# Squared-ReLU attention and gated block: seven-product sums for 6 instead of 4 of 12 column blocks, in-place squares, half-batch values, one list of units

## The chip, the cores and the metric

The kernel runs on one core of a Trainium2 chip. The metric is device time in microseconds for one execution. Before the change the median of three runs is 408.92 us (408.41 to 411.5).

## The reference

```python
# attention: batch 8, heads 12, sequence 448, head size 64
scores = matmul(q, k.transpose(0, 1, 3, 2)) / sqrt(64)
attn = maximum(scores, 0) ** 2 / 448
x = matmul(attn, v)          # laid out as (3584 tokens, 768)
# gated block: w_gate, w_val (768, 1536), w_out (1536, 768)
g = x @ w_gate
gelu = 0.5 * g * (1 + erf(g / sqrt(2)))
out = (gelu * (x @ w_val)) @ w_out
```

All inputs and the output are float32; the kernel loads them as bf16 and accumulates in float32.

## The kernel before

Work goes by batch of 448 tokens. Every matmul uses one 64x64 quarter of the TensorE array (`mm`, L299): two row halves, called PE0 and PE1 in the code, and two column halves, so that four matmuls can run side by side.

For each batch there are 21 score units (`add_scores`, L597). Each fills one PSUM tile `sp` with the scores of 896 columns; ACT takes the ReLU of it (L634, tile `rl`), DVE squares two units at once (a *duo*, L646, tile `attnT`). Six value units (`add_values`, L678) multiply the squares by v; each gives 128 of the 768 rows of x transposed, copied and scaled into `xT` (L709 on DVE or L720 on ACT). q and k of a third of a batch (4 heads) are transposed on TensorE for batches 0 and 1 (L567), and from batch 2 on by a regrouping copy on DVE (L402, `qkr`) and a transposing DMA on SP's queue (L407, `qkT`).

The gate and value products have 12 column blocks of 128 per batch. A dense block of one batch is two units (`add_gate_value`, L901) of 24 matmuls of 448 columns each: the gate unit ends in a gelu on ACT (L922), the value unit in a multiplication on DVE (L927), which writes the block into `uT`. From batch 2 on (`ALONE = 2`) two neighbouring batches form a pair, and for the first 4 blocks (`2 * NP`, `NP = 2`) both batches together are computed as a 2x2 block product in seven units (`add_pair`, L795) of 12 matmuls. These use sums of weights (`add_pair_sums`, L755, `ws`) and sums of x (`add_token_sums`, L773, `ts`). Units 1, 6, 5 and 3 accumulate one after another in one PSUM bank (stage X), 7 and 4 in a second (Y), 2 in a third (Z). After each unit the bank is read: 1, 6 and 7 are copied to `part` on ACT (L843), 2, 4 and 5 are added to `part` on DVE (L847), gelus are taken on ACT (L851) and multiplied on DVE (L856). The first unit of a stage waits for all six values of the second batch (L835).

The output product goes over 14 groups of 256 tokens (`add_product`, L1042), each in seven units of 24 matmuls of 384 columns, with weight sums (`add_weight_sums`, L948, L961), sums of `uT` (`add_sums`, L986, L1026), copies to `osb` on ACT (L1110), additions on DVE (L1108) and stores on SP's queue (L1125). `uT` has room for two batches, so writing batch b waits until the products of batch b - 2 have read theirs.

The order is made before anything runs. `run_plan` (L74) simulates the engines with the costs and lags written in the code and emits instructions in the order of its simulated time. TensorE's units come from a list `later`, sorted by a due time `at`: from the first 40 (`AHEAD`) it takes the first that is ready, or else the one that is ready soonest (`next_unit`, L108). The text `LINE` (L12) gives the order of the gate, value, pair and product units; a digit is the next dense unit of that batch, `2A1` is unit 1 of block A of the pair starting at batch 2, and `a7` is unit 7 of output group a. Score and value units get their due times from a formula and the numbers in `SHIFT` (L1209 to L1239). There are 6 PSUM banks for products and one score tile, once the second score tile has been given up early in the run.

Loads are issued on POOL's queue in the order of L1141 to L1171: batches 0 and 1 mixed with the gate and value weights, then the output weights, then batches 2 to 7 by thirds, each held back until its buffer is free and until a given ReLU has run.

```python
load_w12(4)
load_w12(5)
for i in range(FC // WOG):
    load_wo(i)
add_weight_sums()

late = [(b, m) for b in range(2, B) for m in range(NM)]
```

Of the kernel before, what the change touches and what calls it, by code (L numbers as in the profile page):

```python
# [12 lines left out]
0 0 0 0 0 0 0 0 0 0 0 0 0 a7 0 0 0 0 0 1 1 0 0 1 0 1 0 1 0 1 0 1 1 1 a1 1 1 b1 1 2 a6 a4 a5 1 1 c1 1  # L13
1 1 1 2 1 1 1 a2 2 1 a3 1 1 c6 b6 c7 b7 b5 b2 2 2 c4 2 2 c5 2 2 b3 b4 2 2 3 c2 2A1 2A6 2A7 3 2B1 3
c3 2A2 2B7 2 3 3 2A5 2 2B2 2 2B6 3 2B5 2D1 2D2 2B4 3 2 2C1 2C2 2 3 3 2A3 2C7 2D7 2C6 2B3 2D6 2D5 3
2A4 2D3 2C4 2D4 3 d1 3 3 d6 d7 3 e7 d2 d5 e1 e2 3 e6 e4 d4 2C5 d3 e5 4 4 2C3 3 4 f1 e3 f2 f7 f6 f4
g1 g7 4 f5 g6 g5 4 4 g3 4 g2 4 f3 4B1 5 4 4 5 5 4B2 5 5 4A1 4A2 4B7 g4 4 4B6 4A7 5 4 4 4 4B5 5 4 4
4D1 4A6 5 4C1 4C2 4C6 4D2 4D7 5 5 4C7 4D6 4C5 4D5 5 4C4 4B4 4D4 4A5 5 4A4 i1 4B3 h7 5 h1 5 4D3 h6
4A3 5 4C3 5 h2 i2 h5 i6 h3 i7 6B1 6 j1 6 6B2 6A1 h4 6 6A7 7 i5 6B7 j2 6 6D1 6 6B6 6 6 i3 6A2 7 6 7
i4 7 6 6 6A6 6B5 6 7 6D6 6 7 6 6C7 j7 6 6D2 6D7 j6 6D5 7 6C1 7 j5 6B3 6D3 6A5 6C6 6C2 6C5 6 j4 6D4  # L20
k1 6C4 6 6B4 7 j3 6C3 6A4 k7 l7 l1 7 7 k6 6A3 7 k2 l6 l5 l3 k5 k3 l4 k4 l2 7 7 7 m1 7 n1 m7 m6 n7 m5
n6 m4 m2 n4 n5 m3 n3 n2
# [3 lines left out]
SHIFT = "8 1 7 -2 1.5 1 2.5 -15 5 -3.5 -2.5 -5.5"  # L26


class Op:


    def __init__(self, engine, cost, emit, deps=(), lag=0.0, prio=0, other=None):
        self.engine, self.cost, self.emit, self.prio = engine, cost, emit, prio
        self.deps = [d for d in deps if d is not None]
        self.lag = lag
        self.other = other
        self.takes = None
        self.margin = 0.0
        self.after = None
        self.start = self.end = self.known = self.blocked = None  # L40


class Ring:


    def __init__(self, size, lag=0.0):
        self.size, self.lag, self.ends, self.keys = size, lag, [], set()

# [6 lines left out]
    def take(self, last, key=None):  # L55
        if key is None or key not in self.keys:
            self.ends.append(last)
            self.keys.add(key)


class Unit:


    def __init__(self, at, los, his, box=None, closer=None, prev=None):
        self.at, self.los, self.his, self.box, self.closer, self.prev = at, los, his, box, closer, prev
        self.begun = False
        self.short = False


AHEAD = 40  # L70
BANK = 0.3


def run_plan(queues, pools, units, banks, arrivals, together, fill):  # L74

# [5 lines left out]
    units.sort(key=lambda u: u.at)  # L81
    fixed = len(queues["PE0"])

    def ready(op):
        if op.known is not None:
            return op.known
        if op.blocked is not None and op.blocked.end is None:
            return None
        t = 0.0
        if op.after is not None:  # L90
            if op.after.start is None:
                return None
            t = op.after.start
        if op.takes is not None:
            x = op.takes[0].free(*op.takes[2:])
            if x is None:
                return None
            t = max(t, x)
        for d in op.deps:
            if d.end is None:  # L100
                op.blocked = d
                return None
            t = max(t, d.end + d.lag + (op.margin if d.engine == "SP" else 0.0))
        if op.takes is None:
            op.known = t
        return t

    def next_unit(short):  # L108
        best = None
        now = max(free["PE0"], floor)  # L110
        for u in units[:AHEAD]:
# [3 lines left out]
            if t is None:  # L115
                continue
# [29 lines left out]
    left = sum(map(len, queues.values())) + sum(len(u.los) + len(u.his) for u in units)  # L146
    left += len({id(op) for ops in pools.values() for op in ops})
    while left:
# [16 lines left out]
        for e, ops in pools.items():  # L165
            mine = None
            for op in ops[:48]:
                r = ready(op)
                if r is not None:
                    t = max(r, free[e], floor if e in together else 0.0)  # L170
                    key = (t, op.prio, free[e])
                    if mine is None or key < mine[0]:
                        mine = (key, e, op)
            if mine and (best is None or mine[0] < best[0]):
                best = mine
        assert best is not None, "the plan is stuck"
        (t, _, _), e, op = best
        if isinstance(op, tuple):
            _, u, k = op
            u.begun = True  # L180
            units.remove(u)
            if k is not None:
# [3 lines left out]
            pools["PE1"] += u.his  # L186
# [16 lines left out]
        else:  # L203
            pools[e].remove(op)
            if op.other is not None:
                for x in ("ACT", "DVE"):
                    if x != e:
                        pools[x].remove(op)
        if op.takes is not None:
            op.takes[0].take(*op.takes[1:])  # L210
        op.emit()
        last = max(last, op.end)
# [5 lines left out]
def kernel(  # L218
# [10 lines left out]
    nc = tc.nc  # L229
# [10 lines left out]
    NM = NPAIR // 2  # L240
    NU = SC * NPAIR // 2
# [24 lines left out]
    xpool = ctx.enter_context(tc.tile_pool(name="xpool", bufs=2))  # L266
    upool = ctx.enter_context(tc.tile_pool(name="upool", bufs=2))
    tpool = ctx.enter_context(tc.tile_pool(name="tpool", bufs=RING_T))
    lpool = ctx.enter_context(tc.tile_pool(name="lpool", bufs=2))
    hpool = ctx.enter_context(tc.tile_pool(name="hpool", bufs=RING_H))  # L270
    spool = ctx.enter_context(tc.tile_pool(name="spool", bufs=2))
    rpool = ctx.enter_context(tc.tile_pool(name="rpool", bufs=RING_R))
# [3 lines left out]
    npool = ctx.enter_context(tc.tile_pool(name="npool", bufs=1))  # L276
# [8 lines left out]
    warm = npool.tile([128, 3 * 512], bf16, name="held", tag="held")[:, 0:512]  # L285
# [107 lines left out]
    def add_dma_transposes(b, m, deps=()):  # L393
# [21 lines left out]
        copy = Op("DVE", 0.62, emit_copy, [wait, *(regrouped[n - 2] if n > 1 else ())], lag=0.15, prio=1)  # L415
# [41 lines left out]
    def next_scores(at):  # L457

        n = len(units)
        if at > WIDE and n % SB == 0 or wide:  # L460
            if not wide:
                wide.append(0)
                until.update({FB: at, FB + 1: at})
# [28 lines left out]
    def both(at, ops, scores=False):  # L492

        ops = list(ops)
        if at > FIXED:
# [3 lines left out]
            later.append(Unit(at, [lo for lo, _ in ops], [hi for _, hi in ops], prev=last_scores[0]))  # L499
# [7 lines left out]
    def then(at, step, los, his, box=None, closer=None):  # L507

        if not isinstance(at, list) and at > FIXED:
# [3 lines left out]
            later.append(Unit(at, los, his, box, closer))  # L513
# [35 lines left out]
    def add_transposes(at, b, m, rs):  # L549
# [23 lines left out]
        n, last = next_scores(at) if b else (0, [])  # L573
# [19 lines left out]
        both(at, both_ops)  # L593
# [3 lines left out]
    def add_scores(at, b, u):  # L597
# [7 lines left out]
        n, free = next_scores(at)  # L605
# [25 lines left out]
        def emit_relu():  # L631
            if first:
                duo["rl"] = rpool.tile([128, 2, 2, S], bf16, name="rl", tag="rl")
            relu.ins = nc.scalar.activation(  # L634
                duo["rl"][:, u % 2, :, :], box[0][:, :, 0:S], AF.Relu).ins

        def emit_sq():
            if alone and not first:
                a = duo["a"]
            else:  # L640
                a = duo["a"] = apool.tile([128, 2, 2, S], bf16, name="attnT", tag="attnT")
# [4 lines left out]
            nc.vector.tensor_tensor(a[:, part], duo["rl"][:, part], duo["rl"][:, part], op=ALU.mult)  # L646
# [26 lines left out]
        both(at, zip(*ops))  # L673
# [4 lines left out]
    def add_values(at, b, pr):  # L678
# [24 lines left out]
        def x_tile():  # L703
            if b not in xT:
                xT[b] = xpool.tile([128, KC, S], bf16, name="xT", tag="xT")
            return xT[b][:, pr, :]
# [29 lines left out]
        else:  # L736
            then(at, 0.0, *ops, box, lambda: x_op[b, pr])
# [10 lines left out]
    PLACE5 = -7.0  # L748

    ws, ws_op, ts, ts_op, ts_used = {}, {}, {}, {}, {}  # L750
    K3 = KC // 2
    KTOP, KEND = slice(0, K3), slice(K3, KC)
    ALONE = 2

    def add_pair_sums(i):  # L755

        for n in (1, 2, 4):
# [602 lines left out]
```

## Time and profile before

| What | Value |
|---|---|
| Median of three runs | 408.92 us |
| Span of the profiled execution, first to last instruction | 406.2 us |
| Mean granted TensorE clock | 0.997 |
| TensorE busy | 396.6 us, 8554 matmuls |
| TensorE weight loads | 349.0 us |
| VectorE (DVE) busy | 282.1 us, 480 instructions |
| ScalarE (ACT) busy | 240.7 us, 359 instructions |
| GpSimd (POOL) busy | 73.7 us |
| DMA | 44.86 MB, 110 GB/s on average |

The page gives no time of its own for the profiled execution beside its span; the median of the timed runs is 2.7 us longer than that span. Busy times are shares of the same 406.2 us, and the engines work side by side. A TensorE record lasts from a matmul's start to its modelled end, and several overlap, so "busy" says only that at least one was under way. In the lists, a line number is that of the code, a name such as `ff<-xT,wg` is the written tile and the read ones, and the brackets behind an instruction give the idle time ahead of it on its engine and what ended it.

### The profile page before, as it was taken

How to read it: one execution, taken by the hardware profiler on the slowest of the kernel's cores; microseconds unless marked ns; L12 is line 12 of the kernel's file. 1: busy time of each engine (PE TensorE's matmuls, PEld its weight loads, DVE VectorE, ACT ScalarE, POOL GpSimd, SP SyncE). 2: the span in 40 equal slices, each digit the busy share in tenths (PEclk: the TensorE clock that was granted, in tenths of full speed). 3: DMA queues.
4: the chain of work that ended last, by engine and by line, in shares of the span. 5: the costliest groups of instructions: out<-in, count | busy, mean ns of one | idle time of the engine just before them, and what ended most of it. 6: DMA issues, size and time to landing. Idle time of an engine off the chain costs nothing.

```text
span 406.2 us, 18670 instructions
## 1 busy us (share of the span) xinstructions
PE 396.6 (98%) x8554; PEld 349.0 (86%) x8554; DVE 282.1 (69%) x480; ACT 240.7 (59%) x359; POOL 73.7 (18%) x120
## 2 busy tenths in 40 slices
PE   7899999999999999999999999999999999999995
PEld 3457788889998888999999999998999889889994
DVE  3884787549896688869677787658786765566352
ACT  5856872276676778885556678666546744443130
POOL 7655520211212122121111212020110000000000
PEclk9999999999999999999999999999999999999998
DMA  7999999979899999964779699471323302100416
GB/s 103 184 199 198 197 210 163 120 107 133 108 149 178 165 154 106 110 88 58 96 139 144 113 184 146 69 115 33 48 30 81 79 4 55 29 2 4 135 27 157
DMA packets 75279, 44.86 MB, mean 110 GB/s; under 512 B 36160, under 2 KB 71744, under 8 KB 75200
## 3 DMA queue, kind: packets, MB, share of 16 engines
q0 software_dynamic: 37152, 24.39, 44.9%
q1 hardware_dynamic: 37888, 19.08, 27.2%
q8 instruction: 67, 1.10, 1.1%
q10 hardware_dynamic: 160, 0.20, 0.2%
q14 instruction: 12, 0.10, 0.1%
HBM read 48.76 MB, written 11.01 MB: 147 GB/s over the span
## 4 chain that ended last, share of the span: by engine, by line
PE 93%; DMA 4%; POOL 1%; ACT 0%; issue 0%; SPq 0%; POOLq 0%
PE ff L300 83%; PE sp L300 8%; DMA qkT<-qkr 2%; DMA qk<-in_k_dram 2%; PE ff L488 1%; PE sp L567 1%; POOL qk L355 1%; PE ff L567 1%; ACT rl L634 0%; ACT gel L922 0%; ACT osb L1110 0%; POOL ident masks.py:199 0%; POOL ident masks.py:197 0%; SPq L407 0%; POOLq L1344 0%
## 5 line engine op out<-in xcount | busy, mean ns | idle before, releaser
L300 PE MATMUL ff<-xT,wg 64*64 64x448 bf16 x2016 | 210.1, 349 | 0.0
L300 PE MATMUL ff<-xT,wv 64*64 64x448 bf16 x1728 | 191.1, 349 | 0.0
L634 ACT ACTIVATE rl<-sp 128x896 bf16<-128x896 f32 x168 | 151.9, 921 | 53.5 <-PE sp L300 47.8
L300 PEld LDWEIGHTS <-wv 64*64 64x64 bf16 x2016 | 122.0, 107 | 10.5
L300 PEld LDWEIGHTS <-wg 64*64 64x64 bf16 x2016 | 121.6, 106 | 10.6
L646 DVE TENSOR_TENSOR attnT<-rl 128x1792 bf16<-128x1792 bf16 (+1 forms) x98 | 91.8, 953 | 17.8 <-ACT rl L634 16.2
L300 PE MATMUL ff<-attnT,v 64*64 64x448 bf16 (+1 forms) x768 | 85.8, 326 | 0.3
L300 PEld LDWEIGHTS <-s 64*64 64x64 bf16 x1344 | 77.8, 107 | 2.5 <-issue 0.3
L300 PE MATMUL sp<-qkT 64*64 64x448 bf16 (+1 forms) x768 | 73.4, 328 | 1.5 <-DMA qkT<-qkr 0.8
L922 ACT ACTIVATE gel<-ff 128x448 bf16<-128x448 f32 x72 | 39.1, 543 | 48.0 <-PE ff L300 47.8
L927 DVE TENSOR_TENSOR uT<-gel,ff 128x448 bf16<-128x448 bf16 x72 | 44.4, 619 | 31.6 <-PE ff L300 24.5
L300 PE MATMUL ff<-wo,s 64*64 64x384 bf16 x672 | 61.3, 323 | 0.0
L300 PE MATMUL ff<-wt,s 64*64 64x384 bf16 x672 | 54.9, 323 | 0.0
L300 PE MATMUL ff<-wo,uT 64*64 64x384 bf16 x576 | 54.8, 322 | 0.0
L300 PEld LDWEIGHTS <-uT 64*64 64x64 bf16 x912 | 53.5, 107 | 1.4
L370 POOL DMA_DIRECT2D v<-in_v_dram x48 | 29.5, 619 | 128.2 <-ACT rl L634 49.1
L300 PEld LDWEIGHTS <-v 64*64 64x64 bf16 x768 | 46.5, 107 | 6.2 <-issue 2.5
L1110 ACT COPY osb<-ff 128x384 f32<-128x384 f32 x56 | 26.8, 479 | 37.9 <-PE ff L300 35.8
L300 PEld LDWEIGHTS <-qkT 64*64 64x64 bf16 x768 | 36.2, 106 | 9.0 <-issue 4.8
L709 DVE TENSOR_SCALAR xT<-ff 128x448 bf16<-128x448 f32 x48 | 29.7, 622 | 13.4 <-PE ff L300 12.7
L1108 DVE TENSOR_TENSOR osb<-ff,osb 128x384 f32<-128x384 f32 x42 | 23.4, 556 | 18.4 <-PE ff L300 15.0
L300 PE MATMUL ff<-ts,ws 64*64 64x448 bf16 x288 | 33.4, 349 | 0.0
(57 smaller groups left out, 340.0 us busy)
## 6 DMA issues: line engine op xcount, KB each, us to landing
out_dram<-osb SPq DMA_DIRECT2D x54, 192.0 KB, 3.6
v<-in_v_dram POOLq DMA_DIRECT2D x48, 128.0 KB, 5.1
qk<-in_q_dram POOLq DMA_DIRECT2D x23, 224.0 KB, 5.3
qk<-in_k_dram POOLq DMA_DIRECT2D x23, 224.0 KB, 6.4
wg<-in_moe_w_gate_dram POOLq DMA_DIRECT2D x6, 384.0 KB, 10.2
wv<-in_moe_w_val_dram POOLq DMA_DIRECT2D x6, 384.0 KB, 11.2
wo<-in_moe_w_out_dram POOLq DMA_DIRECT2D x4, 576.0 KB, 14.9
qkT<-qkr SPq DMA_TRANSPOSE x36, 5.2
```

The source lines that it names most:

```text
L300: return nc.tensor.matmul(o, lhsT, rhs, start=start, stop=stop, skip_group_check=onto, tile_position=(P * row, P * col))
L355: op = load(4 * (h1 - h0) * S * D, lambda: nc.gpsimd.dma_start(tile_of(), src[b, h0:h1].rearrange("h (p c) d -> p h (c d)", c=SC)), deps, ...
L370: return nc.gpsimd.dma_start(v16[b, m][HALF[i], :, :, :], v[b, h0:h1].rearrange("h (p c) d -> p h c d", c=SC)[:, :, c0:c0 + VC, :])
L488: nc.tensor.matmul(t[:, :], warm[:, 0:128], warm[:, :], start=True, stop=True)
L567: nc.tensor.transpose(t[HALF[j], c, :], src[:, 2 * r + j, c, :], ident[:, :], tile_position=(0, P * j))
L634: relu.ins = nc.scalar.activation(duo["rl"][:, u % 2, :, :], box[0][:, :, 0:S], AF.Relu).ins
L646: nc.vector.tensor_tensor(a[:, part], duo["rl"][:, part], duo["rl"][:, part], op=ALU.mult)
L709: nc.vector.tensor_scalar_mul(x_tile(), box[0][:, 0:S], scalar1=out_scale)
L922: nc.scalar.activation(gel[b, fc][:, :], box[0][:, 0:S], AF.Gelu)
L927: u_op[b, fc].ins = nc.vector.tensor_tensor(uT[b][:, fc, :], gel.pop((b, fc))[:, :], box[0][:, 0:S], op=ALU.mult).ins
L1108: ins = nc.vector.tensor_tensor(o, box[0][:, 0:OGS], o, op=ALU.add)
L1110: ins = nc.scalar.copy(o, box[0][:, 0:OGS])
```

## The change

- `NP` goes from 2 to 3: blocks 0 to 5 of each pair are computed in seven units, and blocks 6 to 11 densely.
- ReLU writes into the `attnT` tile, and DVE squares it there. The `rl` tiles are gone; a ReLU waits for the values that read its buffer last. Batch 0 has a ring of 5 such buffers in a pool that is later given to the new weight sums and to the token sums; after that the ring is 4.
- `xT` is kept in half batches in a ring of 5 instead of whole batches in a ring of 2.
- The output weights are loaded ahead of the third (2, 2) on POOL's queue, behind the q and k of thirds (2, 0) and (2, 1) and v of (2, 0).
- The copies to `part` and to `osb` may go to ACT or to DVE, by the planner's choice.
- `LINE` now holds every unit behind the start, `s` being the next score unit and `o` the next value unit; the due times and `SHIFT` are gone. The planner takes units from the first 60 of the list and skips those whose buffers could not come free in the order chosen so far.

```diff
-0 0 0 0 0 0 0 0 0 0 0 0 0 a7 0 0 0 0 0 1 1 0 0 1 0 1 0 1 0 1 0 1 1 1 a1 1 1 b1 1 2 a6 a4 a5 1 1 c1 1
...
+0 1 4A1 s 1 s 1 0 o 2 5 1 1 o d1 s 4C5 1 1 1 0 o 0 0 c5 s 2C1 s s o 3 s 0 s a1 s 0 1 2B4 o 5 2 g2
+o s 3 0 2 b7 s 1 o 6B6 o s s s a5 a7 s 4B1 2 d4 s 0 0 0 0 o s 0 a2 4D1 2C7 s s s o 2E1 2A5 0 2C6 s
...
-SHIFT = "8 1 7 -2 1.5 1 2.5 -15 5 -3.5 -2.5 -5.5"
-AHEAD = 40
+AHEAD = 60
 BANK = 0.3
+SPARE = 1
...
             t = ready(u.los[0])
             if t is None:
                 continue
+            if any(op.takes[0].stuck(op.takes[2] if len(op.takes) > 2 else None, sure, n)
+                   for n, op in enumerate(u.grabs)):
+                continue
+            if any(not x.begun for op in u.wants for x in units_under(op) if x is not u):
+                continue
+            if u.chain is not None and u.box is not None and len(opened) >= len(banks) - SPARE:
+                continue
...
+    WO_AT = 2, 2, 2, 2
 
-    NP = 2
-    RING_V, RING_T, RING_H, RING_R, RING_A, RING_O = 3, 3, 2, 2, 4, 4
-    RING_M, RING_G = 5, 4
+    NP = 3
+    RING_V, RING_T, RING_H, RING_L, RING_A, RING_O, RING_E = 3, 3, 2, 2, 4, 4, 5
+    RING_M, RING_G, RING_X = 5, 4, 5
...
         def emit_relu():
             if first:
-                duo["rl"] = rpool.tile([128, 2, 2, S], bf16, name="rl", tag="rl")
+                duo["a"] = (apool if b else sb["first"]).tile([128, 2, 2, S], bf16, name="attnT", tag="attnT")
             relu.ins = nc.scalar.activation(
-                duo["rl"][:, u % 2, :, :], box[0][:, :, 0:S], AF.Relu).ins
+                duo["a"][:, u % 2, :, :], box[0][:, :, 0:S], AF.Relu).ins
...
-            nc.vector.tensor_tensor(a[:, part], duo["rl"][:, part], duo["rl"][:, part], op=ALU.mult)
+            nc.vector.tensor_tensor(a[:, part], a[:, part], a[:, part], op=ALU.mult)
...
-        old = duos[n_d - RING_R] if n_d >= RING_R else None
-        relu = Op("ACT", 0.845, emit_relu, [ops[0][-1], ops[1][-1], *(old["sq"] if old else ())],
-                  lag=0.18, prio=2)
+        relu = Op("ACT", 0.845, emit_relu, [ops[0][-1], ops[1][-1]], lag=0.18, prio=2)
...
-            if b not in xT:
-                xT[b] = xpool.tile([128, KC, S], bf16, name="xT", tag="xT")
-            return xT[b][:, pr, :]
+            h, dc = divmod(pr, K3)
+            if (b, h) not in xT:
+                xT[b, h] = xpool.tile([128, K3, S], bf16, name="xT", tag="xT")
+            return xT[b, h][:, dc, :]
...
         if name in "167":
-            rd = Op("ACT", 0.5, emit_copy, [last], lag=0.2, prio=0)
+            rd = Op("ACT", 0.5, emit_copy, [last], lag=0.2, prio=0,
+                    other=("DVE", 0.58, lambda: emit_copy(nc.vector.tensor_copy)))
...
         rd = Op(engine, 0.52 if added else 0.45, emit_read,
-                [ops[1][-1], *([st["read", before]] if before else ())], lag=0.2, prio=0)
+                [ops[1][-1], *([st["read", before]] if before else ())], lag=0.2, prio=0,
+                other=None if added else ("DVE", 0.52, lambda: emit_read(nc.vector.tensor_copy)))
...
-    for i in range(FC // WOG):
-        load_wo(i)
-    add_weight_sums()
-
     late = [(b, m) for b in range(2, B) for m in range(NM)]
     for n, (b, m) in enumerate(late):
+        for i in range(FC // WOG):
+            if WO_AT[i] == n:
+                load_wo(i)
         for i in range(2):
             load_qk(b, i, 4 * m, 4 * m + 4)
         for b_, m_ in late[n - 1:n] + (late[n:] if n == len(late) - 1 else []):
             load_v(b_, 4 * m_, 4 * m_ + 4)
+    add_weight_sums()
...
-    for new, old in zip(duos[RING_A:], duos):
+    n = (NU + 1) // 2
+    for new, old in [*zip(duos[RING_E:n], duos), *zip(duos[n + RING_A:], duos[n:])]:
         gone = [o_op[b, pr] for keys in old["of"] for b, pr, _ in keys]
-        for sq in new["sq"]:
-            sq.deps += gone
+        for relu in new["relu"]:
+            relu.deps += gone
...
-        op.deps += reads_x.get(b - 2, ())
+        op.deps += reads_x.get(old_half(b, pr), ())
...
+    for u in later:
+        if u.name[0] == "o":
+            b = u.name[1]
+            u.los[0].gates += reads_x.get(old_half(b, u.name[2]), ())
+        elif u.name[0] == "p" and u.name[2] in "17":
+            u.los[0].gates += [u_op[b, f] for tile in sums[u.name[1]]["chunks"] for b, _ in tile for f in range(FC)]
```

More of the change, by code (lines that the diff above doesn't have):

```diff
@@ L39, in __init__ @@
         self.after = None
[L40 removed]
+        self.gates = []
+        self.start = self.end = None
+        self.place = 0
+        self.open = False
 class Ring:
@@ L181, in run_plan @@
             units.remove(u)
+            for x in u.grabs:
+                x.takes[0].ask(*x.takes[1:])
+            if u.chain is not None:
+                opened.add(u.chain)
+                if u.name[-1] in "234":
+                    opened.discard(u.chain)
             if k is not None:
@@ L203, in run_plan @@
         else:
[L204 to L208, printed above, removed]
+            for x in homes[op]:
+                able[x].remove(op)
         if op.takes is not None:
@@ L1178 @@
+    for at, _, fn, args in work:
+        fn(at, *args)
+    names = {}
+    for u in later:
+        names.setdefault(u.name[:2] if u.name[0] == "o" else u.name, []).append(u)
+    flow = {str(b): [("g", *x) for x in dense[b]] for b in range(B)}
+    flow["0"] = flow["0"][2:]
+    flow["s"] = [("s", b) for b in range(B) for _ in names.get(("s", b), ())]
+    flow["o"] = [("o", b) for b in range(B) for _ in names.get(("o", b), ())]
     line = []
```

375 lines of the change are left out of this document (223 added, 152 removed).

## The prediction

> **What bounds the kernel now.** I read the page's first and fourth parts, the timeline of an undisturbed stretch, the groups by shape, and the busy time by windows, in that order. The page says that TensorE is busy almost throughout and that the chain that ended last runs over it for 93% of the span:
>
> ```profile
> span 406.2 us, 18670 instructions
> ...
> PE 396.6 (98%) x8554; PEld 349.0 (86%) x8554; DVE 282.1 (69%) x480; ACT 240.7 (59%) x359; POOL 73.7 (18%) x120
> ...
> PE 93%; DMA 4%; POOL 1%; ACT 0%; issue 0%; SPq 0%; POOLq 0%
> ```
>
> A busy PE is not a full PE here, because a matmul uses one 64x64 quarter of the array and four can run together. The timeline gives the price when all four do (start, duration, instruction):
>
> ```profile
> 67.57 0.38 PE L300 MATMUL ff<-xT,wg 64*64 64x448 bf16 x2
> ...
> 67.61 0.35 PE L300 MATMUL ff<-xT,wv 64*64 64x448 bf16 x2
> ...
> 67.76 0.38 PE L300 MATMUL ff<-xT,wg 64*64 64x448 bf16 x2
> ...
> 67.80 0.35 PE L300 MATMUL ff<-xT,wv 64*64 64x448 bf16 x2
> ```
>
> Each half of the array starts a new pair every 0.19 us, so a 64x448 matmul costs 0.19 / 4 = 47 ns of the array although its record is 349 ns long. By columns, a 384-column one costs 40.5 ns. The counts by shape (5616 of 448 columns, 384 of 224, 2352 of 384) then make 265 + 9 + 95 = 369 us, and the transposes some 6 us more: 375 us of real work up to the last matmul at 401. So about 26 us are lost. The windows (length, PE busy and records, PEld, DVE, ACT, POOL, clock) show where:
>
> ```profile
> 20.00:30.00 10.00, 9.85 (x152) 5.47 (x149) 8.22 (x16) 5.73 (x8) 5.79 (x9) 1.00 1.38 199
> 30.00:40.00 10.00, 10.00 (x210) 7.49 (x207) 4.77 (x8) 5.50 (x8) 5.80 (x9) 1.00 1.40 199
> 80.00:82.00 2.00, 1.19 (x28) 0.87 (x21) 0.13 (x1) 0.54 (x1) 0.00 (x0) 1.00 0.75 105
> 145.00:150.00 5.00, 5.00 (x118) 4.55 (x112) 3.56 (x6) 3.42 (x5) 0.61 (x1) 1.00 1.19 236
> 150.00:155.00 5.00, 4.87 (x74) 3.02 (x68) 4.45 (x8) 3.44 (x5) 1.62 (x3) 1.00 0.71 72
> 155.00:160.00 5.00, 5.00 (x114) 4.91 (x113) 4.80 (x8) 4.28 (x8) 0.82 (x2) 1.00 1.18 159
> ```
>
> By columns the first 30 us lose 12.7 us to loads and to batch 0's chain of scores, squares and values. Beyond that, 30 to 60 loses 2.5, the wait at 81 us 1.1, 70 to 80 0.6, 150 to 155 1.9 (74 records against 118 and 114 beside it), 270 to 280 0.8. Everywhere else the loss is 0.1 to 0.3 in 10 us: the middle is nearly full, and only less work or fewer of these named gaps shorten it. Two gaps have a plain cause:
>
> ```profile
> 82.04 0.57 PE L300 MATMUL sp<-qkT 64*64 64x448 bf16 x8 [0.85 <-DMA qkT<-qkr]
> ```
> ```profile
> 153.39 0.92 ACT L634 ACTIVATE rl<-sp 128x896 bf16<-128x896 f32 x1 [0.48 <-PE sp L300]
> ...
> 154.78 0.92 ACT L634 ACTIVATE rl<-sp 128x896 bf16<-128x896 f32 x1 [0.48 <-PE sp L300]
> ```
>
> At 81 the first scores of batch 2 wait for the transposing DMA. At 150 to 155 the scores and ReLUs take turns on the one score buffer, one unit in 1.4 us, and too little other work is put between them.
>
> **The change, part by part.** *Two more column blocks in seven products, for three pairs of batches (six cases).* A dense block of a pair takes 4 x 24 = 96 matmuls, a seven-product one 7 x 12 = 84. Saved: 6 x 12 = 72 at 47 ns, **3.4 us of PE**, certain as work, and on the path wherever PE is full. What it adds stands on the other engines:
>
> ```profile
> L927 DVE TENSOR_TENSOR uT<-gel,ff 128x448 bf16<-128x448 bf16 x72 | 44.4, 619 | 31.6 <-PE ff L300 24.5 <-ACT gel L922 3.9 <-ACT rl L634 2.6
> L922 ACT ACTIVATE gel<-ff 128x448 bf16<-128x448 f32 x72 | 39.1, 543 | 48.0 <-PE ff L300 47.8
> ...
> L847 DVE TENSOR_TENSOR part<-ff,part 128x448 f32<-128x448 f32 x36 | 21.7, 621 | 12.3 <-PE ff L300 9.1 <-ACT part L843 3.0
> L843 ACT COPY part<-ff 128x448 f32<-128x448 f32 x36 | 18.9, 532 | 7.8 <-PE ff L300 7.4
> ...
> L851 ACT ACTIVATE gel<-part 128x448 bf16<-128x448 f32 x12 | 6.9, 577 | 0.8 <-DVE part L847 0.8
> ```
>
> The two gelus and two multiplications stay (one gelu at 577 for 543 ns). Three copies (3 x 0.532) and three additions (3 x 0.621) come on top: 1.63 us of ACT and 1.86 of DVE a case, 9.8 and 11.2 in all. One more set of weight sums is four DVE operations at 0.55: 2.2 us. DVE goes from 282 to about 295, ACT from 241 to about 250, of 406: hidden under PE's work on average; the cover is gone where DVE is at 9 of 10 already (90 to 120). There a late copy holds a bank, and the next of its seven products waits. Bounds 0 and 13.5 us (worked out under the slow rival); I take 1.0, near nothing, since the copies may now go to either engine and both idle over 100 us.
>
> [...]
>
> *Squares in place.* The same 98 operations on the same shapes; no row shows an in-place one. Price 0 by these rows; bounds -4 (the 4.1 us that ReLU waited for squares, at L634, were all on the path) and +4 (ReLU now waits for the values that last read its buffer, a ring of 4 duos where 2 and 4 stood one behind the other). Behind a waiting ReLU on ACT stand the gelus and the bank copies, and for these wait L927 on DVE and the next product of the bank. I take 0, in the middle of the two.
>
> *Values in half batches.* Same copies, 2.5 batches of room for 2: nothing added; bounds 0 and -0.8 (the gap at 270).
>
> *Output weights later.* Four issues on POOL (0.75 each, 14.9 us to landing) are moved behind the q and k loads of thirds (2,0) and (2,1) and v of (2,0). These issued at 48.4 to 60.0 behind the weights' 42.8 to 47.9, so q and k of (2,0) come up to 5.5 us sooner, and with them DVE's regrouping copies, SP's transposes and the scores at 82. Gain up to 1.1. What becomes late: the eight output weight sums (0.75 each, at 63.8 to 71.9) and the first products (68.4) move back by some 10 us. That hides behind the 48 gate and value units of batches 0 and 1 (1.13 us each, 54 us of PE from 26 on, plus 16 us of attention); without that cover it would cost up to 10.
>
> *One searched list.* Scores and values are now placed by the list and no longer by a formula and shifts. No operation is added; the new gates hold only the planner's choice and are no waits on the chip. It can take away at most the named gaps, 2.5 + 0.6 + 1.1 + 1.9 + 0.8 = 6.9, less the 0.15 in 10 us that any stretch loses: 6.0 (the 1.1 at 81 among them). Bounds -6 and +4 (two more gaps like that at 150). I take half the gain, -3.5: the gap at 81 (shorter DMA wait) and that at 150 (scores spread) are the plainest.
>
> Sum, from the median 408.9 (the span 406.2 and 2.7 around it, which stay): -3.4 + 1.0 - 3.5 = **403.0 us**. The start, up to batch 0's values and the first two gate units, is untouched, and so are the 5 us of last copy and stores.
>
> **Rivals.**
> (1) *Arithmetic only*: the new order makes as many gaps as it closes, 408.9 - 3.4 = **405.5**. For it: the middle is nearly full already. Against: 150 to 155 is a gap of order, not of work.
> (2) *Slower: the start of each pair runs out of cover.* The first seven-product unit of a pair waits for all values of the second batch (L835). With six blocks for four, the first batch offers 2 x 2 gate and value units fewer to fill the gaps between its partner's scores: 4.5 us a pair, three pairs, 13.5 us if nothing else is ready, while PSUM banks are held for three more copies a case. From 7.5 us lost it decides for slower by over 1%; I price it at 10: 408.9 - 3.4 + 10 = **415.5**. For it: exactly this shape at 150 to 155, where 5 us lose 1.9. Against: products of the pair before (6.8 us for each of 14 groups) are also cover. [...]
> (3) *All gaps close*: -3.4 - 6.0, **399.5**. Against: 30 to 60 still has its loads at 200 GB/s.
> (4) *The blocks are regrouped, but PE's time does not fall*, because the four quarters are no longer fed evenly: no row of the middle shows that, and it lands within rival 1.
>
> **How the numbers follow.** Forecast (400.5 to 404.8) 0.45, (3) 0.12, (1) with (4) 0.25, (2) 0.18. 1% is 4.1 us, about what a measurement tells from no change, so faster begins under 404.8: 0.57; same 0.25; slower 0.18. The range 399.5 to 412 leaves about 0.05 below and 0.15 above.
>
> **What would show it.** PE records fall from 8554 by 72, apart from fill matmuls; copies into part go from 36 to 54, on ACT or DVE. Right: no window after 30 us like that of 74 records in 5 us, the wait for qkT at 81 gone, the last matmul near 395. Wrong: ACT's ReLU waiting for PE in 1.4 us steps ahead of each pair, gel or part on ACT waiting for DVE, or PE waiting for part, for the output weight sums or for attnT.

## The result: slower by 0.75%, and the profile after

The changed kernel takes 412.16 us (median, 410.87 to 414.84), the kernel before, measured again beside it, 409.07 us; the ratio is 1.0075 with a 95% interval of 1.0055 to 1.0095. The forecast was 403.0 us. In the profiled executions the span goes from 406.2 to 410.1 us and the mean granted clock from 0.997 to 0.985.

The page of the changed kernel, its span, busy times and chain:

```profile
span 410.1 us, 18547 instructions
...
PE 392.3 (96%) x8477; PEld 348.1 (85%) x8480; DVE 298.5 (73%) x513; ACT 244.8 (60%) x366; POOL 74.1 (18%) x120
...
PE 91%; DMA 5%; ACT 1%; issue 1%; DVE 1%; SPq 0%; POOL 0%; POOLq 0%
```

TensorE has 77 records fewer (the 72 of the change and 5 fill matmuls, products without use that the kernel puts into idle time at the start). It is busy for 4 us less and yet the span is 4 us longer. Of the chain that ended last, 5% are now transfers (4% before); the page's list by line gives the transposing DMA `qkT<-qkr` 4%, before 2%. The windows (length, PE busy and records, PEld, DVE, ACT, POOL, clock, DMA share, GB/s) show where that is:

```profile
70.00:75.00 5.00, 0.00 (x0) 0.12 (x1) 0.56 (x1) 0.00 (x0) 0.00 (x0) 0.55 1.24 173
75.00:80.00 5.00, 2.47 (x28) 1.56 (x31) 0.00 (x0) 1.73 (x2) 0.61 (x1) 0.50 0.74 104
80.00:85.00 5.00, 5.00 (x106) 4.20 (x101) 4.16 (x7) 2.24 (x4) 0.61 (x1) 0.92 1.00 122
```
```profile
150.00:155.00 5.00, 5.00 (x116) 4.46 (x111) 3.49 (x7) 3.81 (x6) 1.22 (x2) 1.00 0.91 169
```

From 70 to 75 us not one matmul starts. The stretch that answers to the gap of before at 150 is full: 116 records instead of 74. The waits (waiter, what it waited for, us in total, times, longest) name the hole, and so does the timeline where it ends:

```profile
PE sp L375 <- DMA qkT<-qkr: 9.0, 1, 9.0
...
PEld L375 <- DMA qkT<-qkr: 5.2, 1, 5.2
```
```profile
77.53 0.96 PE L375 MATMUL sp<-qkT 64*64 64x448 bf16 x8 [9.01 <-DMA qkT<-qkr]
78.23 0.63 PE L375 MATMUL ff<-xT,wg 64*64 64x448 bf16 x2
...
78.60 0.63 PE L375 MATMUL ff<-xT,wg 64*64 64x448 bf16 x2
```

The first scores of batch 2 wait 9.0 us for their transposing DMAs, and the gate and value work that stands behind them in TensorE's order starts only after them. When it goes on, a half of the array starts a pair every 0.37 us instead of 0.19: the granted clock is 0.50, and only comes back near 80.8. That is 3.2 us at half speed, another 1.6 us. The transposes themselves, in the list by tile of the changed kernel:

```profile
L482 SPq DMA_TRANSPOSE qkT<-qkr x36: 1211/1242/7292, 58.2 to 296.1; - x36
...
DMA to landing us min/median/max: 2.7/5.3/17.9
```

The kernel before has 7.9 us there as its longest, from a first issue at 72.1:

```profile
DMA to landing us min/median/max: 2.7/5.2/7.9
```

What filled most of the 17.9 us is seen in the DMA queues of the changed kernel between 64 and 68 us (packets, MB, share of the 16 engines' time; q0 carries POOL's loads, q1 what SP issues; packets of the two overlap, so the shares add up to more than 100%):

```profile
q0 software_dynamic: 466, 0.69, 93.9%
q1 hardware_dynamic: 464, 0.12, 22.1%
```

In these 4 us the two queues move as many packets as each other, 466 and 464, as if they took turns, but a packet of the output weights takes 134 ns and a transpose's 31. Alone, the transposes' queue moved up to 821 packets in a microsecond (at 79); here it got 116. Whether a turn is one of these packets or several in a row, the trace does not show.

The turns do not explain the start. Nothing of the transposes moved before 62 us, 3.9 us after SP had issued the first one at 58.2, while POOL's loads, from 58.8 on the output weights alone (issued at 52.0 to 56.2), filled the engines. With the engines idle the first packet came 1.3 us after the issue (kernel before, 72.1). Why the other 2.6 us passed without a turn stays open.

The account of the whole run counts each matmul at about the price of the prediction (46.7 ns for 448 columns when four run together, by columns for the others) and calls the rest of a stretch lost (us). The differences between the versions hardly depend on this price. The last version is e10_copy_behind_square:

| | before | after | after, no weight loads | last version |
|---|---|---|---|---|
| matmul work, fill included | 375.1 | 370.7 | 371.4 | 370.7 |
| lost 0 to 30 | 12.7 | 12.3 | 11.9 | 13.2 |
| 30 to 60 | 2.5 | 2.5 | 2.6 | 2.5 |
| 60 to 90 | 2.05 | **11.1** | 5.6 | 2.3 |
| 90 to 150 | 1.2 | 2.0 | 2.5 | 2.0 |
| 150 to 270 | 4.0 | 1.85 | 1.9 | 2.4 |
| 270 to 390 | 2.3 | 2.4 | 2.4 | 2.7 |
| 390 to the end | 6.2 | 7.2 | 7.0 | 6.7 |
| span | 406.2 | 410.1 | 405.2 | 402.5 |

The third and fourth columns are experiments below.

### The profile page after: what moved, and what is told of

It is laid out like the page before. It is cut to its first block, busy times and chain, and to the rows that moved or that the text cites. A ratio compares the mean times of both kernels' runs of the same rounds, so it can differ in the third digit from the quotient of the medians.

```text
span 410.1 us, 18547 instructions
## 1 busy us (share of the span) xinstructions
PE 392.3 (96%) x8477; PEld 348.1 (85%) x8480; DVE 298.5 (73%) x513; ACT 244.8 (60%) x366; POOL 74.1 (18%) x120
## 4 chain that ended last, share of the span: by engine, by line
PE 91%; DMA 5%; ACT 1%; issue 1%; DVE 1%; SPq 0%; POOL 0%; POOLq 0%
PE ff L375 80%; PE sp L375 8%; DMA qkT<-qkr 4%; PE ff L562 1%; ACT attnT L708 1%; PE sp L641 1%; DMA qk<-in_k_dram 1%; PE ff L641 0%; DVE qkT L645 0%; DVE attnT L717 0%; PE ff L604 0%; ACT gel L1002 0%; DVE osb L1196 0%; SPq L482 0%; ACT qkT L612 0%
## 5 line engine op out<-in xcount | busy, mean ns | idle before, releaser
L375 PE MATMUL ff<-xT,wg 64*64 64x448 bf16 x1872 | 195.4, 351 | 0.0
L708 ACT ACTIVATE attnT<-sp 128x896 bf16<-128x896 f32 x168 | 151.6, 922 | 55.8 <-PE sp L375 53.4
L375 PE MATMUL ff<-xT,wv 64*64 64x448 bf16 x1440 | 156.3, 352 | 0.2 <-issue 0.2
L375 PEld LDWEIGHTS <-wg 64*64 64x64 bf16 x1872 | 113.7, 107 | 9.0 <-issue 0.2
L717 DVE TENSOR_TENSOR attnT<-attnT 128x1792 bf16<-128x1792 bf16 (+1 forms) x98 | 92.3, 953 | 12.6 <-ACT attnT L708 11.9
L375 PE MATMUL sp<-qkT 64*64 64x448 bf16 (+1 forms) x768 | 79.7, 330 | 10.1 <-DMA qkT<-qkr 9.0
L1007 DVE TENSOR_TENSOR uT<-gel,ff 128x448 bf16<-128x448 bf16 x60 | 37.0, 617 | 31.2 <-PE ff L375 27.0
L375 PE MATMUL ff<-ts,wv 64*64 64x448 bf16 x432 | 51.5, 349 | 0.0
L375 PE MATMUL ff<-ts,ws 64*64 64x448 bf16 x432 | 51.1, 349 | 0.0
L375 PEld LDWEIGHTS <-ws 64*64 64x64 bf16 x648 | 41.1, 106 | 2.3
L924 DVE TENSOR_TENSOR part<-ff,part 128x448 f32<-128x448 f32 x54 | 32.9, 620 | 11.8 <-PE ff L375 7.0
## 6 DMA issues: line engine op xcount, KB each, us to landing
wo<-in_moe_w_out_dram POOLq DMA_DIRECT2D x4, 576.0 KB, 13.5
```

Of the source, the lines that this page charges most:

```text
L375: return nc.tensor.matmul(o, lhsT, rhs, start=start, stop=stop, skip_group_check=onto, tile_position=(P * row, P * col))
L708: relu.ins = nc.scalar.activation(duo["a"][:, u % 2, :, :], box[0][:, :, 0:S], AF.Relu).ins
L717: nc.vector.tensor_tensor(a[:, part], a[:, part], a[:, part], op=ALU.mult)
L924: rd.ins = nc.vector.tensor_tensor(t[:, :], box[0][:, 0:S], t[:, :], op=ALU.add).ins
L1007: u_op[b, fc].ins = nc.vector.tensor_tensor(uT[b][:, fc, :], gel.pop((b, fc))[:, :], box[0][:, 0:S], op=ALU.mult).ins
```

## The experiments

The theory: the output weights, moved later, are in the DMA engines when the first transposes of batch 2 want to pass, and this alone turns a gain into a loss. The rivals: the new order itself issues the transposes too early for any arrangement of loads; or the loss at 70 only hides a loss of cover that seven products for more blocks bring. In most experiments the order of the changed kernel on TensorE, VectorE, ScalarE and SyncE was kept as it was, so that only the named thing moves. The ratios are to the kernel before, run beside each experiment; the spans, losses and waits come from one profiled execution each. For e9_sums_behind_values (410.21 us) and e6_split_small (413.0) that execution was 2.4 and 2.8 us longer than the median, for e4_wo_first (419.8) 3.6 us shorter.

| Experiment | median us | ratio to before, 95% | span us |
|---|---|---|---|
| e1_no_wo_load | 406.57 | 0.9912 [0.9877, 0.9946] | 405.2 |
| e2_wo_small_packets | 407.86 | 0.9968 [0.9939, 0.9997] | 405.7 |
| e3_plan_lag18 | 423.82 | 1.0339 [1.0293, 1.0384] | 421.7 |
| e4_wo_first | 423.43 | 1.0328 [1.0275, 1.0381] | 418.0 |
| e5_wo_split_wait | 406.60 | 0.9934 [0.9893, 0.9975] | 404.4 |
| e6_split_small | 410.17 | 1.0014 [0.9974, 1.0053] | 411.2 |
| e7_before_wo_late | 417.98 | 1.0175 [1.0104, 1.0246] | 416.0 |
| e8_gate_on_first | 408.02 | 0.9967 [0.993, 1.0004] | 407.1 |
| e9_sums_behind_values | 407.81 | 0.9932 [0.9901, 0.9963] | 408.4 |
| e10_copy_behind_square | 404.96 | 0.9886 [0.984, 0.9932] | 402.5 |

**e1_no_wo_load**: the order kept, the weights not loaded; POOL writes zeros in their place.

```diff
-        wo_op[i] = load(4 * WOG * 128 * d_model, lambda: nc.gpsimd.dma_start(
-            wo[i][:, :, :], moe_w_out[rows, :].rearrange("(c p) f -> p c f", p=128)))
+        wo_op[i] = load(4 * WOG * 128 * d_model, lambda: nc.gpsimd.memset(
+            wo[i][:, :, :], 0.0))
```

> The changed kernel in its own order on every engine, with the four loads of the output weights left out: GpSimd fills those tiles with zeros in their place (so the products with the output weights are not those of the reference). Theory A (the 9.0 us wait at 68 to 77 comes from the output weights' bytes, which share the DMA engines with the first transposes of batch 2): the transposes of (2,0), issued at 58 to 60, land in about 5 to 8 us instead of 17.9, the wait is under 2 us, no half clock behind it, and the span falls from 410.1 to 399 to 402. Theory B (the wait is the list's: the first scores of batch 2 simply stand too early, or q and k come late): the wait stays above 5 us and the span at 406 or more. Theory C (the other parts of the change cost the time): the span stays at 408 or more.

The longest landing falls from 17.9 to 10.1 us and the span by 4.9. That is the direction of the theory, but less than it expected: a wait is left.

```profile
PE sp L375 <- DMA qkT<-qkr: 2.9, 1, 2.9
```

In the DMA queues of this run, 64 to 68 us, the loads of q, k and v of the next thirds now stand beside the transposes:

```profile
q0 software_dynamic: 539, 0.43, 97.3%
q1 hardware_dynamic: 325, 0.08, 36.6%
```

So the output weights make about 5.5 of the 9 us that are lost more at 60 to 90. The 3.5 that are left are put down to the other loads by subtraction alone.

**e2_wo_small_packets**: the order kept, each weight load cut into three of 256 columns, so that its packets are a third as long.

```diff
+        wo_op[i] = load(4 * WOG * 128 * d_model, lambda: [nc.gpsimd.dma_start(wo[i][:, :, c:c + WCH], moe_w_out[rows, c:c + WCH].rearrange(
+            "(c p) f -> p c f", p=128)) for c in range(0, d_model, WCH)][-1])
```

> The changed kernel in its own order, each load of output weights cut into three of 256 columns, so that its packets are 512 B long instead of 1536 B, for the same bytes. Theory A in its narrow form (the transposes' packets and the load's packets take turns one for one on each DMA engine; 134 ns for a long one, 60 for one of 512 B): the transposes of (2,0) run about 204 packets a us instead of 114 and land in 12 to 14 us instead of 17.9, the wait falls from 9.0 to 3 to 6 us, and the time by 3 to 6 us. Theory A in a broad form (they share bytes, not turns): the landing and the time stay within 1.5 us of the changed kernel. Theories B and C: no change.

The same bytes in shorter packets: the landing falls to 12.3 us and TensorE's longest wait to 3.5. In the DMA queues of this run, 64 to 68 us, the turns are again one for one, but there are twice as many of them:

```profile
q0 software_dynamic: 907, 0.45, 86.8%
q1 hardware_dynamic: 901, 0.23, 52.6%
```

The packets' length was changed, and with it POOL's issues (12 for 4), so that the loads behind the weights were also issued 7 to 8 us later. The doubled count beside the same kind of load shows that the turns set the transposes' rate; how much of the 5.6 us came from the later loads is not shown apart. The landing, the wait and the time are those that the narrow theory had named.

**e7_before_wo_late**: the kernel before, its list and sizes, with only the weights' place in POOL's queue changed; the planner made its order anew.

```diff
-    for i in range(FC // WOG):
-        load_wo(i)
-    add_weight_sums()
...
     for n, (b, m) in enumerate(late):
+        if n == 2:
+            for i in range(FC // WOG):
+                load_wo(i)
+            add_weight_sums()
```

> The kernel before with one part of the change alone: the output weights loaded behind q and k of (2,0) and (2,1) and v of (2,0), its own list and shifts, planned anew. Theory A: the transposes of (2,0) start about 10 us earlier, under the weights' loads, land in 12 to 18 us, and the time grows by 2 to 12 us wherever TensorE has no other work ready, 411 to 421. If this list keeps other work ahead of batch 2's scores (as it does at 74 to 82 today), the slow transposes cost nothing and the time is within 2 us of 409.

The moved loads make the kernel before 1.75% slower (1.0 to 2.5%), with the same hole (windows and waits of this run):

```profile
70.00:80.00 10.00, 2.42 (x34) 1.44 (x29) 1.96 (x4) 1.92 (x3) 0.16 (x1) 0.73 1.02 121
```
```profile
PE sp L300 <- DMA qkT<-qkr: 7.6, 1, 7.6
```

The transposes are issued at 60.5 instead of 72.1, because q and k come sooner, and land at 78. From 60 to 90 us 10.0 us are lost, against 2.05 before. That is 7.9 of the 9.8 us by which the span grows; the other 1.9 are spread over the run, and the new order may have its part in them.

**e4_wo_first and e3_plan_lag18**: the changed kernel with the weights back in front of (2, 0), and with the planner told that the transposes of (2, 0) land 18 us late. Both are ordered anew.

```diff
-    WO_AT = 2, 2, 2, 2
+    WO_AT = 0, 0, 0, 0
```

> The changed kernel with the output weights loaded where they were before, ahead of q and k of (2,0), the list unchanged (the planner orders the units anew). Theory A: the transposes of batch 2 start when the big loads are done, land in 5 to 8 us, the wait is at most 2 us, and the time is 8 to 11 us below the changed kernel: 401 to 404, so below the kernel before by 5 to 8. Theory B: the list was searched for the late weights and fits the early ones worse; 405 to 411. Theory C: 408 or more.

```diff
-                          [copy], lag=5.0) for c0, c1 in ((0, VC), (VC, SC))]
+                          [copy], lag=18.0 if (b, m) == (2, 0) else 5.0) for c0, c1 in ((0, VC), (VC, SC))]
```

> The changed kernel with one number of its planner altered: the transposes of (2,0) are planned with a lag of 18.0 instead of 5.0 us, nothing else is moved by hand (the planner orders the units anew from there). Theory A: the transposes land as late as before (14 to 18 us), but TensorE has other work in front, so the wait at 68 falls under 3 us and the time by 5 to 10 us, to 402 to 407. Theory B': there is no other work that could run, since the first products need the late output weights: the wait only moves or is shared out, and the time stays within 3 us of 412. Theory C: at least 409.

In e4_wo_first the transposes land in at most 7.5 us, and in neither run does TensorE wait at 68. Yet both are 3.3% slower than the kernel before, where theory A had expected a gain; by the time alone both would speak for theory C (the other parts of the change cost the time), and against it speak e1_no_wo_load, e5_wo_split_wait and e10_copy_behind_square, which have all these parts in the kept order. What they lose, they lose elsewhere, after the order was made anew; that the list of units no longer fits the new course of events is the reading, not a separate test. The windows of e4_wo_first and ACT's timeline there:

```profile
110.00:115.00 5.00, 3.20 (x44) 1.63 (x40) 3.33 (x8) 3.85 (x5) 0.61 (x1) 1.00 1.05 183
115.00:120.00 5.00, 3.90 (x35) 2.37 (x34) 2.26 (x3) 2.27 (x4) 1.22 (x2) 0.52 0.78 123
```
```profile
101.64 0.92 ACT L708 ACTIVATE attnT<-sp 128x896 bf16<-128x896 f32 x1 [0.48 <-PE sp L375]
103.04 0.92 ACT L708 ACTIVATE attnT<-sp 128x896 bf16<-128x896 f32 x1 [0.48 <-PE sp L375]
```

Scores and ReLUs take turns in 1.40 us steps with nothing else ready, the shape of rival 2: 90 to 150 loses 13.6 us in e4_wo_first and 16.9 in e3_plan_lag18, against 2.0. In both tries the list of the change did badly with another order of events. For an experiment this means that a new plan moves more than the thing under test; hence the kept order elsewhere.

**e5_wo_split_wait**: the order kept on four engines; on POOL the weights of blocks 0 and 2 go first, and those of 1 and 3 and the next loads wait until the transposes of (2, 0) have landed.

```diff
+            if op in late_ops and not landed:
+                return put_off.append(paced)
...
-            for d in op.behind:
+            for d in [*op.behind, *(landed if op in late_ops else ())]:
...
+            if (b, m) == (2, 0) and c0:
+                landed.append(ins)
+                for issue in put_off:
+                    issue()
```

> The changed kernel in its own order on every engine but one swap on GpSimd's queue: output weights 0 and 2 are issued first, and weights 1 and 3 and the loads behind them (q and k of third (2,2), v of (2,1)) wait until the transposes of (2,0) have landed. Theory A (shared DMA engines): from about 64 us on the transposes have the engines for themselves and land at 66 to 69 instead of 77.5; the wait of 9.0 us shrinks to under 1.5, no half clock follows, the first weight sums at 69 are not delayed by more than 1 us. Time 8 to 10.5 us under the changed kernel: 401.5 to 404, 1.2 to 1.8% faster than the kernel before. If what is put off (weights 1 and 3, v of (2,1)) is needed sooner than I think, a new wait of 2 to 6 us shows between 75 and 95, and the time is 405 to 409. Theory C (the other parts cost the time): not below 406.

The transposes land at 67.3 and the wait at 68 is gone; 60 to 70 loses 0.3. The weights held back are now late themselves (DVE's and then PE's timeline):

```profile
78.76 0.76 DVE L1057 TENSOR_TENSOR wt<-wo,wo 128x1152 bf16<-128x1152 bf16 x1 [5.87 <-DMA wo<-in_moe_w_out_dram]
```
```profile
80.77 0.38 PE L375 MATMUL ff<-xT,wg 64*64 64x448 bf16 x2 [2.08 <-DVE uT L1017]
85.17 0.38 PE L375 MATMUL ff<-attnT,v 64*64 64x448 bf16 x2 [1.33 <-DVE attnT L727]
```

VectorE stands 5.9 us in front of a weight sum, and behind it stand the product and the square for which TensorE waits. 70 to 90 loses 4.1 us. Still, this version is 0.7% faster than the kernel before (0.25 to 1.1%), where the changed kernel is 0.75% slower.

**e6_split_small**: e5_wo_split_wait with the short packets of e2_wo_small_packets.

> The same as the run before it, and the output weight loads are cut into three of 256 columns each (packets of 512 B). Theory A in the narrow form, packets taking turns: the transposes, which start under weights 0 and 2, get ahead sooner, land 1 to 3 us earlier than in the run before, and if that run still has a wait this one has less of it: within 1 us of it or up to 2 us faster. Against it: twelve issues of 0.75 us for four may delay weights 1 and 3 by 2 to 4 us.

The expectation failed: 410.17 us, the transposes landed at 70.3, 3 us later and not 1 to 3 earlier, and VectorE's wait for the weights grew from 5.9 to 7.7 us. By the row of e2_wo_small_packets above, a short packet of the loads' queue took 61 ns (86.8% of 64 us for 907 packets), so three of them take 184 ns for the bytes of one long packet of 134. Weights 0 and 2 landed at 69.7 instead of 65.7. Here the short packets cost more than they gave.

**e8_gate_on_first**: e5_wo_split_wait, held back until the first of the two transposes has landed.

```diff
-            if (b, m) == (2, 0) and c0:
+            if (b, m) == (2, 0) and not c0:
```

> The changed kernel with its order on TensorE, VectorE, ScalarE and SyncE kept. GpSimd issues the output weights of blocks 0 and 2 where they were; those of blocks 1 and 3, and behind them the loads of q, k of (2, 2) and v of (2, 1), wait until the first of the two transposes of (2, 0) has landed, not both as in e5_wo_split_wait. There the second landed at 67.3 us and the weights of 1 and 3 began to move at 69.7; VectorE waited 5.9 us for them and the stretch 70 to 90 lost 4.1 us. If packets of two queues taking turns set both times, the weights start near 65 to 66 and run partly beside the rest of the transposes: second landing 68 to 70 us, TensorE's wait for it 0 to 2 us, VectorE's wait for the weights 1 to 3 us, loss from 70 to 90 of 1.5 to 3 us, and a time of 403.5 to 405.5 us. If what the transposes lose is what the weights win, one for one, the sum stays: 406 to 407.5 us. If TensorE's loss in e5_wo_split_wait did not come from VectorE's wait, the loss of 70 to 90 stays at 4 us or more even with a wait under 3 us.

The rival in which the weights win what the transposes lose came nearest, and the time lies just above its band: 408.02 us. The last weights landed 1.9 us sooner and VectorE's wait fell only to 4.9; they now ran beside the transposes of (2, 1), which came late in their turn (a wait of 2.0 us at 86.7), and 80 to 90 lost 5.2 us.

**e9_sums_behind_values**: e5_wo_split_wait, with the first two sums of blocks 1 and 3 moved behind the next two products on VectorE.

```diff
+                done = Op("DVE", 0.75, (lambda emit=emit: later_wt.append(emit)) if i and n in (3, 2) else emit,
...
+            if later_wt:
+                muls.append(fc)
+                if len(muls) == 2:
+                    for issue in later_wt:
+                        issue()
```

> e5_wo_split_wait with one more move, on VectorE: the first two of the four weight sums of blocks 1 and 3 stand behind the next two products of gelu and value and the score block between them, so that what waits for the late output weights is no longer ahead of what TensorE's rows wait for. All else is in the order of the changed kernel. If TensorE's loss of 4.1 us from 70 to 90 in e5_wo_split_wait came from VectorE standing 5.9 us in front of its queue, the wait becomes 0 to 2 us, the loss of that stretch 0.5 to 2 us and the time 403 to 405 us (span 401 to 403). The next thing that could be late is TensorE's own first product with the weights of block 1, at 81 us in e5_wo_split_wait, which needs them by about 79; they landed at 78.8, so at most 1 us. If the loss stays near 4 us, the late operands of TensorE are set by something else than the weights, and the time stays at 406 to 407.5 us.

VectorE's wait fell to 1.5 us as expected, the time did not fall: 407.81 us, a ratio like that of e5_wo_split_wait. The next thing in VectorE's queue was a regrouping copy whose load was one of those held back (1.5 us of waiting), and behind it the square; TensorE waited 2.6 us for that, once. Later transposes, issued behind that copy, were late too: TensorE waited 1.6 us for them at 98.8, and 90 to 100 lost 2.1 us.

**e10_copy_behind_square**: the same, with that copy moved behind the square.

```diff
+            if (b, m) == (2, 2) and not now:
+                return later_copy.append(lambda: emit_copy(True))
...
+            while later_copy:
+                later_copy.pop()()
```

> e9_sums_behind_values with VectorE's regrouping copy of q, k of (2, 2) moved behind the next square of a score block. In e9_sums_behind_values that copy waited 1.5 us for its load (one of those held back), the square behind it ended late, and TensorE stood 2.6 us at 81.6 to 84.2 for it; the stretch 80 to 100 lost 5.1 us. If that copy was the cause, the 2.6 us go, the stretch 80 to 100 loses 1.5 to 3 us and the time is 404 to 406 us; the transposes of (2, 2) come about 1 us later, which may return up to 1 us. If the square is late because of the weight sums' own 1.5 us of waiting and their 1.5 us of work ahead of it, the loss stays at 4 to 5 us and the time at 407 to 408.5.

404.96 us, faster than the kernel before by 1.1% (0.7 to 1.6) and the lowest ratio here, though its interval overlaps with those of e5_wo_split_wait and e9_sums_behind_values. The windows of this run and TensorE's waits from 66 to 100 us (its timeline):

```profile
60.00:70.00 10.00, 10.00 (x224) 8.70 (x220) 7.34 (x13) 5.41 (x10) 2.12 (x3) 1.00 0.96 142
70.00:80.00 10.00, 9.93 (x218) 8.38 (x214) 6.31 (x10) 6.87 (x10) 4.33 (x8) 1.00 1.14 175
80.00:90.00 10.00, 8.91 (x201) 7.42 (x195) 9.85 (x16) 4.84 (x8) 1.22 (x2) 1.00 1.37 167
```

```profile
82.18 0.38 PE L375 MATMUL ff<-attnT,v 64*64 64x448 bf16 x2 [0.84 <-DVE attnT L729]
84.74 0.35 PE L375 MATMUL ff<-wt,s 64*64 64x384 bf16 x1 [0.25 <-issue]
```

All parts of the change are in it, with its list. Only six loads, two weight sums and one copy stand elsewhere, and the loss from 60 to 90 is 2.3 us, as in the kernel before (2.05).

## Why the prediction was wrong

**Output weights later** is the step that failed. It counted four issues on POOL, the later weight sums and the later first products, and promised that q and k of (2, 0) come "up to 5.5 us sooner", with a gain of up to 1.1 us that the sum counts in the list's term; in the sum the step itself stood at nothing. The issues of q and k of (2, 0) did come sooner, by 5.4 and 6.3 us, but with no weights ahead of them in the engines the loads of (2, 0) and (2, 1) landed 12.2 us sooner (57.4 for 69.7), and the transposes were issued 13.9 us sooner (58.2 for 72.1). The step did not ask what else is in the 16 DMA engines by then. The rows for it lay in the trace of before: POOL's loads fill the engines until about 69 us, and the transposes of (2, 0) are issued behind them. Even there only their first 2.3 us were quiet, and they took 6.8 and 7.9 us beside the next, shorter packets of q, k and v; the queues of the kernel before from 74 to 78 us:

```profile
q0 software_dynamic: 512, 0.43, 69.4%
q1 hardware_dynamic: 631, 0.15, 48.2%
```

The change puts the transposes beside the output weights, and they get a turn each behind packets four times as long. Price: 9.1 us more lost in 60 to 90 (11.1 for 2.05). The wait itself is 9.0 us and the half clock after it costs about 1.6. e7_before_wo_late shows that this part makes the hole in the kernel before too, e1_no_wo_load that without the weights more than half of it goes, and e10_copy_behind_square that other places in the queues remove it whole. The cover "behind the 48 gate and value units" was reckoned for the late weight sums and first products, and for these TensorE has no wait in the changed kernel. For late transposes nothing was reckoned, and the same units could not cover them: they stood behind the waiting scores in TensorE's own queue.

**Two more blocks in seven products**, -3.4 us: right as work. The 72 matmuls at 46.7 ns are 3.36 us, and no stretch loses as much more in their place once the hole is gone. In the last version the span is 3.7 us below that of before, but that this is so near to 3.4 is partly luck: 1.1 us less fill and the gaps closed by the list are in it as well, and so is some 1.0 us more at the start and the end.

**Extra evictions** (the readings of PSUM banks that come on top), +1.0 with bounds 0 and 13.5: nothing of it is seen. The groups of the changed kernel for them:

```profile
L924 DVE TENSOR_TENSOR part<-ff,part 128x448 f32<-128x448 f32 x54 | 32.9, 620 | 11.8 <-PE ff L375 7.0 <-ACT part L920 2.5 <-ACT gel L1002 1.6
...
L920 ACT COPY part<-ff 128x448 f32<-128x448 f32 x36 | 19.0, 532 | 18.0 <-PE ff L375 13.0 <-DVE uT L933 4.6
...
L920 DVE COPY part<-ff 128x448 f32<-128x448 f32 x18 | 11.2, 621 | 4.4 <-PE ff L375 4.1
```

The copies are 54, 18 of them on VectorE. The planner also moved other work: 22 copies to `osb` went from ACT to DVE (12.2 us there) and 29 of 48 copies to `xT` from DVE to ACT (15.8 us there). With the terms of the prediction this gives 298.5 us of DVE instead of the 295 worked out and 244.8 of ACT instead of 250. The new copies and additions run from 158 to 372 us, and there the loss fell (4.25 us from 150 to 390 for 6.3), with VectorE busy for 73% and ScalarE for 60% of the span.

**Squares in place**, 0: right as far as the profile shows. The mean stays at 953 ns, the 4.1 us in which ReLU waited for squares are gone, and ReLU's waits for product banks on TensorE (`ff`), among which the values are, come to 1.5 us in all (1.0 before). This part was not tried alone.

**Searched list**, -3.5: mis-sized. The gap at 150 closed as said: 150 to 270 loses 1.85 for 4.0. But 90 to 150 loses 0.8 more, and the gap at 81 became the hole at 70. Between 90 and 390 us 1.3 us less are lost, in the last version 0.5, where the term promised 3.5 with the gap at 81. That a plan made anew from the same list costs 10 us more (e3_plan_lag18, e4_wo_first) was not foreseen. The stretch from 390 to the end, which the prediction left untouched, loses 1.0 us more; no run looks into that.

**Rivals.** None priced what happened. Rival 2 came near in time (415.5) by another mechanism: no start of a pair lost cover in the changed kernel, so the nearness is luck. Its shape showed only where the list was ordered anew.

## What to carry to other kernels

A load that is moved in one queue must be placed against what runs in the other queues at its new time: draw up which transfers fill the DMA engines in that stretch, and take a transfer's landing from a stretch with the same neighbours, not from its median. Where an engine waits for transfers of small packets (TensorE here, 9.0 us), try to give them the DMA engines to themselves: hold bulk loads back behind them, then look at what waits for those loads and move it back in its own queue too. Here e5_wo_split_wait alone brought 0.7%, e9_sums_behind_values nothing more, and e10_copy_behind_square 1.1%; that the last is better than the first is likely but not shown, as the intervals overlap. A searched order is part of the measured kernel: try a single change in it with the order kept, and judge a new plan apart.

## What the runs showed of the hardware

- From 64 to 68 us of the changed kernel two DMA queues shared the engines by packets, not bytes: 466 against 464 packets, with 134 ns for a packet of the output weights and 31 for a transpose's. The transposes got 0.12 of 0.81 MB; with weight packets a third as long (e2_wo_small_packets) the counts were 907 and 901, and they got 0.23 of 0.68 MB in the same 4 us.
- A transpose issued at 58.2 us, while POOL's queue had the engines full, moved no packet for 3.9 us. With the engines idle it was 1.3 us (kernel before, 72.1).
- TensorE's granted clock fell to 0.5 at 70.5 us, 2.0 us after the last matmul had ended (68.5), stayed there for 10.2 us and came back at 80.8, 3.2 us after work resumed. A wait of 2.0 us at 86.7 came with half clock in e8_gate_on_first (mean clock 0.86 from 80 to 90 us and 0.97 from 90 to 100, together 3.4 us of it), while one of 2.6 us from 81.6 on did not in e9_sums_behind_values (1.00 from 80 to 100). What decides between the two, these runs do not show.
